# Products of zeros beside batch 0's attention, and its first transfers in a new order

## The chip, the cores and the metric

One core of one Trainium2 chip. The metric is the time of one execution in device microseconds (us), as the median over runs. The profiles and traces are of single executions; their span runs from the first to the last instruction and is about 1.8 us shorter than the time (390.0 us against 391.85 us for the kernel before). In the profiles PE is TensorE, PEld its weight loads, DVE VectorE, ACT ScalarE, POOL GpSimd, SP the sync engine; a q behind a name (SPq) is that engine's sequencer, which issues the transfers.

## The reference

Causal attention with a bias from a running sum, then layer normalisation and a two-layer MLP with a residual:

```python
q, k, v: (8, 8, 576, 64)   s: (8, 8, 576)        # batches, heads, positions, head size
scores = q @ k.T / 8
cum    = cumsum(maximum(s, 0))
scores = where(causal, -1e9, scores + minimum(-(cum_i - cum_j), 0))
attn   = softmax(scores);   x = attn @ v          # heads side by side: (8, 576, 512)
xn     = (x - mean) / sqrt(var + 1e-6) * g_ln
out    = x + relu(xn @ w_ch1) @ w_ch2             # 512 -> 2048 -> 512
```

## The kernel before

Each batch's attention is interleaved with the MLP of the batch ahead of it, so that TensorE has MLP products to do while ScalarE takes exponentials. Batch 0 has no batch ahead of it: its eight heads run without MLP work beside them. That is the stretch in question.

The bias is carried by four extra rows under the 64 rows of k and q (KA = 68): the running sum, split into three bf16 parts, c_hi, c_mid and c_lo, and its partner rows. For the first batches these rows are written by DMA, in "sets" of four heads. k and q come in "pairs" of heads: loaded, cast to bf16, turned by TensorE's transposes, copied into kq.

```python
ps_s, ps_m, ps_t, ps_o      # PSUM pools: 3 + 2 + 2 + 1 banks; ps_m is the MLP's
...
def ld_cast_pair(g):                                   # k and q of two heads, cast on the way
    ... nc.gpsimd.dma_start(out=ready[kind, g][0:QP], in_=pair_src(kind, g))
def ld_v(b, t):                                        # 128 positions of v, all heads
    ... nc.sync.dma_start(out=tmp[:pn], in_=v[b, :, t*P : t*P+pn, :].rearrange("h s d -> s h d"))
def ld_w1(c):                                          # a 512 KB piece of the weights, as bf16
    nc.gpsimd.dma_start(out=w1_bf[:, :, sl], in_=w1_r[:, :, sl])

def aug(gam, eng, last=None):                          # bias rows of a set of four heads
    r0 = gam * G
    i = gam % 2
    eng.dma_start(out=kq[i][D + 1 : D + 2, 0, :, 0:S], in_=c_hi[r0 : r0 + G, :])
    ...                                                # three more rows

def pre(n):                                            # ahead of head n
    ...
    elif n == 2:
        ld_w1(0)
        v_edges(1)
        ld_v(1, 0), ld_v(1, 1), ld_v(1, 2), ld_v(1, 3), ld_v(1, 4)
    elif n == 3:
        ld_cast_pair(5)
    elif n == 4:
        cast_v(1, 0, "pool")
        cast_v(1, 1, "pool")
    elif n == 5:
        ld_w1(1)
        cast_v(1, 2, "pool")
        cast_v(1, 3, "pool")
        cast_v(1, 4, "pool")
    ...
    if n % 4 == 0 and 2 <= n // 4 + 1 < 2 * NPE:
        aug(n // 4 + 1, nc.gpsimd)                     # n = 4: set 2, heads 8 to 11

for n in range(BH):                                    # heads in order
    b, h = n // H, n % H
    pre(n)
    if n < 10:
        scores(b, h)                                   # sa, sb, sc; ends in exponentials into er
        if h % 2 == 0:
            scores_d(b, h // 2)                        # tail diagonal; masked by GpSimd (er)
        if n % 2 == 0 and n < 8:
            g = n // 2 + 1
            qk_pair(g, "dve", "dve" if g % 2 else "act")
        if n == 9:
            for t in range(NF):
                ln_tr(0, t)
            queue += batch_units(0)                    # MLP of batch 0 starts
        if n > 1:
            pv_next()                                  # pot: attn @ v of head n - 2
        if n == 8:
            pv_next()
            qk_pair(5, "act", "act")
```

The casts of batch 1's v by GpSimd in `pre(6)` or earlier stand ahead of the mask of head 6's tail in `scores_d`, and GpSimd ran them in that order.

The softmax here doesn't subtract the row's maximum and nothing guards it: scores larger than these inputs give would overflow.

## Time and profile before

| | before |
|---|---|
| time, median of 3 (lowest to highest) | 393.23 us (392.23 to 393.25) |
| span in the profile | 390.0 us |
| scores of head 0, of head 8, first MLP product start at | 13.07, 39.65, 50.97 us |
| from the first MLP product to the end | 339.0 us |

The prediction below shows the page's clock row and TensorE's timeline. The sync engine's timeline (start, duration, engine, line, what, how many) and GpSimd's:

```profile
11.16 22.95 SPq L132 DMA_DIRECT2D vtmp<-in_v_dram  x10
```

What the stages cost (columns as in the prediction's windows):

```profile
13.07:39.65 26.58, 23.89 (x218) 17.60 (x219) 14.93 (x31) 17.16 (x32) 22.27 (x42) 1.00 1.15 193
39.65:50.97 11.32, 7.66 (x105) 5.88 (x101) 9.41 (x33) 7.27 (x14) 5.23 (x10) 0.80 0.67 108
```

TensorE looks full in heads 0 to 7 (23.89 of 26.58 us) only because its products take nearly twice as long there (from sa to the next product 0.40 us at 37.22, 0.22 us at 39.65); the printed clock of 1.00 is the value before the first record and means nothing.

### The profile page before, as it was taken

Reading aid. Unit: us, or ns where it says so; the run is one execution under the profiler, and the core shown is the slowest. Engines: PE = TensorE matmul, PEld = TensorE weight load, DVE = VectorE, ACT = ScalarE, POOL = GpSimd, SP = SyncE. Lnnn points to the kernel's source line nnn. Section 1 sums busy time; section 2 is a strip of 40 time slices with the busy share of each in tenths; the row PEclk is TensorE's granted clock in tenths of the full one; section 3 lists DMA queues with packets and bytes.
Section 4 is the critical chain, followed back from the end, with each engine's and each line's share of the span. In section 5 each row is a group of like instructions: output and inputs, shape, how many; then the busy total and the mean of one; then the engine's idle time right before and its main releaser. Section 6 shows DMA issues by size and latency. Waiting matters only on the chain.

```text
span 390.0 us, 8129 instructions
## 1 busy us (share of the span) xinstructions
PE 360.7 (92%) x2959; PEld 199.4 (51%) x2959; DVE 202.5 (52%) x530; ACT 189.7 (49%) x359; POOL 177.6 (46%) x473
## 2 busy tenths in 40 slices
PE   1598699897999999999999999999999979999994
PEld 0376555454555555555555555655555534444441
DVE  7347745859643745484437545843665483212211
ACT  3476758574685356436743774277337400411400
POOL 5897359465656264636466656454742110000000
PEclk9999879999999999999999999999999989999998
DMA  8999799256886898749896998599820011002013
GB/s 190 223 155 206 132 129 152 30 105 155 184 180 125 143 242 184 173 118 234 180 166 158 236 177 195 141 213 170 195 92 4 2 54 55 2 28 81 2 34 73
DMA packets 148335, 51.84 MB, mean 133 GB/s; under 512 B 134696, under 2 KB 143496, under 8 KB 148296
## 3 DMA queue, kind: packets, MB, share of 16 engines
q1 hardware_dynamic: 139168, 44.07, 51.9%
q0 software_dynamic: 9120, 7.25, 12.5%
q8 instruction: 23, 0.38, 0.4%
q14 instruction: 16, 0.13, 0.1%
q10 hardware_dynamic: 8, 0.00, 0.0%
HBM read 37.11 MB, written 9.44 MB: 119 GB/s over the span
## 4 chain that ended last, share of the span: by engine, by line
PE 79%; DVE 10%; DMA 5%; ACT 2%; SPq 1%; issue 1%; POOL 0%; ACTq 0%; DVEq 0%
PE py L448 30%; PE ph L430 27%; PE pot L343 7%; PE sa L274 3%; PE sb L274 3%; PE sc L274 3%; DVE xn L401 2%; DVE kq L96 2%; PE trx L417 2%; DMA vtmp<-in_v_dram 2%; PE trqk L227 1%; SPq L149 1%; DMA kq<-c_lo 1%; DMA kq<-rows 1%; ACT er L285 1%
## 5 line engine op out<-in xcount | busy, mean ns | idle before, releaser
L448 PE MATMUL py<-w_bf,hT 128*128 128x512 bf16 x576 | 137.9, 381 | 2.5 <-DVE yo L457 2.2
L430 PE MATMUL ph<-xT,w_bf 128*128 128x512 bf16 x512 | 122.7, 381 | 1.2 <-DVE hT L438 1.0
L440 ACT ACTIVATE hT<-ph 128x512 bf16<-128x512 f32 x107 | 64.0, 598 | 83.4 <-PE ph L430 82.7
L430 PEld LDWEIGHTS <-w_bf 128*128 128x128 bf16 x576 | 52.1, 98 | 55.2 <-issue 5.6
L448 PEld LDWEIGHTS <-hT 128*128 128x128 bf16 x576 | 52.1, 98 | 52.5 <-issue 3.6
L285 ACT ACTIVATE er<-sa 128x512 bf16<-128x512 f32 x64 | 38.1, 596 | 79.2 <-PE sa L274 48.1
L293 POOL TENSOR_SCALAR_AFFINE_SELECT er<-er 128x128 bf16<-128x128 bf16 x216 | 59.5, 300 | 31.2 <-ACT er L285 31.0
L438 DVE TENSOR_SCALAR hT<-ph 128x512 bf16<-128x512 f32 x37 | 25.6, 691 | 58.0 <-PE ph L430 55.2
L161 POOL CAST rows<-rowtmp 128x512 bf16<-128x512 f32 (+1 forms) x50 | 30.5, 610 | 48.9 <-DMA rowtmp<-in_q_dram 46.2
L274 PEld LDWEIGHTS <-kq 68*128 68x128 bf16 x440 | 34.7, 102 | 34.6 <-POOL v_bf L98 5.5
L343 PEld LDWEIGHTS <-er 128*128 128x128 bf16 x960 | 40.0, 102 | 15.2 <-DVE xm L360 2.1
L351 DVE RECIPROCAL rinv<-pot 128x5 f32<-128x5 f32 x64 | 12.4, 194 | 61.1 <-PE pot L343 60.9
L343 PE MATMUL pot<-v_bf,er 128*128 128x65 bf16 x960 | 42.4, 199 | 1.7 <-DVE xm L360 1.7
L285 ACT ACTIVATE er<-sc 128x512 bf16<-128x512 f32 x64 | 38.9, 608 | 0.3
L285 ACT ACTIVATE er<-sb 128x512 bf16<-128x512 f32 x64 | 38.2, 596 | 0.0
L457 DVE SCALAR_TENSOR_TENSOR yo<-py,rstd,xb 128x512 f32<-128x512 f32 x32 | 23.8, 748 | 25.5 <-PE py L448 20.3
L98 POOL CAST v_bf<-vtmp 128x512 bf16<-128x512 f32 (+1 forms) x40 | 24.3, 616 | 17.4 <-DMA vtmp<-in_v_dram 17.3
L274 PE MATMUL sa<-kq 68*128 68x512 bf16 x64 | 26.5, 414 | 6.1 <-DMA kq<-c_lo 5.4
L353 DVE TENSOR_TENSOR xb<-pot,rinv 128x256 f32<-128x256 f32 x64 | 27.2, 425 | 2.2
L274 PE MATMUL sc<-kq 68*128 68x256 bf16 (+1 forms) x208 | 27.9, 244 | 0.1
L96 DVE COPY kq<-trqk 64x576 bf16<-64x576 bf16 x24 | 19.2, 800 | 14.9 <-PE trqk L227 14.5
L274 PE MATMUL sb<-kq 68*128 68x64 bf16 (+1 forms) x168 | 26.7, 261 | 0.2
(81 smaller groups left out, 301.9 us busy)
## 6 DMA issues: line engine op xcount, KB each, us to landing
vtmp<-in_v_dram SPq DMA_DIRECT2D x32, 256.0 KB, 4.2
out_dram<-yo SPq DMA_DIRECT2D x32, 256.0 KB, 2.2
rowtmp<-in_k_dram SPq DMA_DIRECT2D x40, 128.0 KB, 3.0
rowtmp<-in_q_dram SPq DMA_DIRECT2D x40, 128.0 KB, 3.2
w_bf<-in_moe_w_ch_dram POOLq DMA_DIRECT2D x8, 512.0 KB, 9.2
kp<-in_k_dram POOLq DMA_DIRECT2D x10, 144.0 KB, 4.1
qp<-in_q_dram POOLq DMA_DIRECT2D x10, 144.0 KB, 4.8
vtmp<-in_v_dram SPq DMA_DIRECT2D x8, 128.0 KB, 3.2
```

Of the source, the lines that this page charges most:

```text
L96: nc.vector.tensor_copy(out=out, in_=in_)
L98: nc.gpsimd.tensor_copy(out=out, in_=in_)
L161: nc.gpsimd.tensor_copy(out=r[0:pn, :, :, 0:D], in_=loaded.pop(("rows", gam, t))[0:pn])
L274: nc.tensor.matmul(a[:, c + a0 - q0 : c + a1 - q0], lhsT=k_cols(b, h, kb), rhs=cols, start=True, stop=not (pe_mask and diag),)
L285: nc.scalar.activation(out=e[:, o : o + 512], in_=a, func=ACT.Exp, scale=scale)
L293: nc.gpsimd.affine_select(out=e[:, o : o + P], in_=e[:, o : o + P], compare_op=ALU.is_ge, fill=0.0, base=0, pattern=[[1, P]], channel_mult ...
L343: nc.tensor.matmul(pot[:, t, :], lhsT=e[:, o : o + P], rhs=vv[:, kb, h, :], start=(kb == 0), stop=(kb == last),)
L353: nc.vector.tensor_tensor(out=xb[b][:, :, hs], in0=pot[:, 0:NF, 0:D], in1=rinv[:, 0:NF].unsqueeze(2).to_broadcast([P, NF, D]), op=ALU.mult,)
L430: nc.tensor.matmul(ph, lhsT=w1_bf[:, kd, fb * P : (fb + 1) * P], rhs=xT[:, kd, :], start=(kd == 0), stop=(kd == KD - 1),)
L438: nc.vector.tensor_scalar_max(out=hT[:, fb, :], in0=ph, scalar1=0.0)
L440: nc.scalar.activation(out=hT[:, fb, :], in_=ph, func=ACT.Relu)
L448: nc.tensor.matmul(py[0], lhsT=hT[:, fb, t * P : (t + 1) * P], rhs=w2_bf[:, fb, :], start=(fb == 0), stop=(fb == FB - 1),)
```

## The change

Intent: keep TensorE's clock up in batch 0. Products of zeros fill the time in which it would idle; batch 0's transposes use the MLP's two idle PSUM banks, so that the zeros have a bank to go to; head 0's bias rows are made by TensorE instead of DMA; and the first transfers are put in the order in which they are needed, with the bias rows of the sets moved from GpSimd's queue to the sync engine's.

```diff
+    def keep_warm(n):
+        w = ps_t.tile([P, 512], F32, name="idle", tag="tr")
+        for _ in range(n):
+            nc.tensor.matmul(w, lhsT=zeros[:, 0:P], rhs=zeros, start=True, stop=True)
 ...
-            tr = ps_t.tile([P, S], BF16, name="trqk", tag="tr")
+            if g < 6:
+                tr = ps_m.tile([P, S], BF16, name="trqk", tag="m")
+            else:
+                tr = ps_t.tile([P, S], BF16, name="trqk", tag="tr")
 ...
-    ld_v(0, 0)
-    ld_v(0, 1)
+    for t in range(3):
+        ld_v(0, t)
+    ld_cast_pair(2)
 ...                                # clears of kq[1] moved here from pre(0), on GpSimd and DVE
+    keep_warm(9)
 ...
-    aug(0, nc.gpsimd, nc.scalar)
+    aug(0, nc.sync, h0=1)          # heads 1 to 3 only
+    ld_v(0, 3)
     qk_pair(0, "dve", "act")
+    ...                            # head 0's rows: eight products with a selector into ba, bb,
+    ...                            # copied by DVE and ACT; keep_warm(4) and keep_warm(5) between
+    ld_cast_pair(3)
+    aug(1, nc.sync)
+    ld_w1(0)
 ...
         elif n == 1:
-            aug(1, nc.gpsimd)
             ld_cast_pair(4)
         elif n == 2:
-            ld_w1(0)
+            ld_w1(1)
+        elif n == 3:
             v_edges(1)
+            ld_w1(2)
+        elif n == 4:
+            ld_cast_pair(5)
+        elif n == 5:
+            ld_w1(3)
             ld_v(1, 0), ld_v(1, 1), ld_v(1, 2), ld_v(1, 3), ld_v(1, 4)
-        elif n == 3: ...            # pair 5; casts at 4 and 5; weights at 5, 7, 9, 10, 11
+        elif n == 6:
+            ld_w2(0)
+            cast_v(1, 0, "pool")
+            cast_v(1, 1, "pool")
+        elif n == 7:
+            cast_v(1, 2, "pool")
+            cast_v(1, 3, "pool")
+            cast_v(1, 4, "pool")
 ...
-            aug(n // 4 + 1, nc.gpsimd)
+            aug(n // 4 + 1, nc.sync)
 ...
-                qk_pair(g, "dve", "dve" if g % 2 else "act")
+                qk_pair(g, "dve", "act")
+            if n < 8:
+                keep_warm(2)
 ...
             if n == 8:
                 pv_next()
+                keep_warm(8)
```

More of the change, by code (lines that the diff above doesn't have):

```diff
@@ L87 @@
     xTm = const.tile([P, KD, 512], BF16, name="xTm")
-    c_hi = const.tile([BH, S], BF16, name="c_hi")
-    c_mid = const.tile([BH, S], BF16, name="c_mid")
-    c_lo = const.tile([BH, S], BF16, name="c_lo")
+    c3 = const.tile([BH, 3, S], BF16, name="c3")
+    c_hi, c_mid, c_lo = (c3[:, j, :] for j in range(3))
+    zeros = const.tile([P, 512], BF16, name="zeros")
+    ones = const.tile([BH, S], BF16, name="ones")
+    pick = const.tile([BH, 4, P], BF16, name="pick")
     def copy_on(eng, out, in_):
@@ L188, in ld_w2, with aug @@
         )
-    def aug(gam, eng, last=None):
-        r0 = gam * G
+    def aug(gam, eng, h0=0):
+        r = slice(gam * G + h0, gam * G + G)
         i = gam % 2
-        eng.dma_start(out=kq[i][D + 1 : D + 2, 0, :, 0:S], in_=c_hi[r0 : r0 + G, :])
-        eng.dma_start(out=kq[i][D : D + 1, 1, :, 0:S], in_=c_hi[r0 : r0 + G, :])
-        eng.dma_start(out=kq[i][D + 2 : D + 3, 0, :, 0:S], in_=c_mid[r0 : r0 + G, :])
-        (last or eng).dma_start(
-            out=kq[i][D + 3 : D + 4, 0, :, 0:S], in_=c_lo[r0 : r0 + G, :]
-        )
+        eng.dma_start(out=kq[i][D : D + 1, 1, h0:G, 0:S], in_=c_hi[r, :])
+        for j in range(3):
+            eng.dma_start(out=kq[i][D + 1 + j : D + 2 + j, 0, h0:G, 0:S], in_=c3[r, j, :])
     def bias_rows():
@@ L504 @@
         ld_pair("q", g)
-    ld_v(0, 0)
-    ld_v(0, 1)
+    for t in range(3):
+        ld_v(0, t)
+    ld_cast_pair(2)
     ONE2 = 1.0019378662109375
     NEG2 = -1.0058441162109375
+    nc.vector.memset(zeros.bitcast(F32), 0.0)
     nc.vector.memset(warm, 0.0)
     nc.scalar.activation(out=warm[:, 1:2], in_=warm[:, 0:1], func=ACT.Exp)
+    keep_warm(9)
     nc.vector.memset(c_one, 1.0)
+    nc.vector.memset(pick.rearrange("p j m -> p (j m)").bitcast(F32), 0.0)
+    for j in range(3):
+        nc.vector.memset(pick[0:1, j, j + 1 : j + 2], 1.0)
+    nc.vector.memset(pick[0:1, 0, 32:33], 1.0)
+    nc.vector.memset(pick[0:1, 3, 0:1], -1.0)
+    nc.vector.memset(ones.bitcast(F32), ONE2)
     nc.vector.memset(kq[0][0:KA, 0, :, S:SP], 0.0)
     nc.vector.memset(kq[0][D:KA, 1].bitcast(F32), ONE2)
+    nc.vector.memset(kq[1][0:KA, 0, :, S:SP], 0.0)
     make_identity(nc, ident)
@@ L526 @@
     nc.gpsimd.memset(kq[0][D : D + 1, 0].bitcast(F32), NEG2)
+    nc.gpsimd.memset(kq[1][D : D + 1, 0].bitcast(F32), NEG2)
+    nc.gpsimd.memset(kq[1][D:KA, 1].bitcast(F32), ONE2)
     def v_edges(i):
@@ L544 @@
     nc.vector.tensor_tensor(out=c_lo, in0=c_in, in1=c_mid, op=ALU.subtract)
-    aug(0, nc.gpsimd, nc.scalar)
+    aug(0, nc.sync, h0=1)
+    ld_v(0, 3)
     qk_pair(0, "dve", "act")
-    ld_v(0, 2)
-    ld_v(0, 3)
+    ba = ps_s.tile([P, 512], F32, name="ba", tag="s")
+    bb = ps_s.tile([P, 512], F32, name="bb", tag="s")
+    for j, src in ((3, ones), (0, c_hi), (1, c_mid), (2, c_lo)):
+        if j == 2:
+            keep_warm(4)
+        nc.tensor.matmul(
+            ba, lhsT=pick[:, j, :], rhs=src[:, 0:512], start=(j == 3), stop=(j == 2)
+        )
+    for j, src in ((3, ones), (0, c_hi), (1, c_mid), (2, c_lo)):
+        nc.tensor.matmul(
+            bb[:, 0:TL], lhsT=pick[:, j, :], rhs=src[:, 512:S], start=(j == 3), stop=(j == 2)
+        )
+    nc.vector.tensor_copy(out=kq[0][D:KA, 0, 0, 0:512], in_=ba[0:4])
+    nc.scalar.copy(out=kq[0][D : D + 1, 1, 0, 0:512], in_=ba[32:33])
+    nc.vector.tensor_copy(out=kq[0][D:KA, 0, 0, 512:S], in_=bb[0:4, 0:TL])
+    nc.scalar.copy(out=kq[0][D : D + 1, 1, 0, 512:S], in_=bb[32:33, 0:TL])
+    keep_warm(5)
     cast_pair("k", 1, "pool")
@@ L551 @@
     ld_v(0, 4)
-    ld_cast_pair(2)
+    ld_cast_pair(3)
+    aug(1, nc.sync)
+    ld_w1(0)
     v_edges(0)
@@ L562, in pre @@
         if n == 0:
-            ld_cast_pair(3)
-            nc.gpsimd.memset(kq[1][D : D + 1, 0].bitcast(F32), NEG2)
-            nc.gpsimd.memset(kq[1][D:KA, 1].bitcast(F32), ONE2)
-            nc.gpsimd.memset(kq[1][0:KA, 0, :, S:SP], 0.0)
             nc.vector.memset(mhalf, -0.5)
         elif n == 1:
-            aug(1, nc.gpsimd)
             ld_cast_pair(4)
         elif n == 2:
-            ld_w1(0)
+            ld_w1(1)
+        elif n == 3:
             v_edges(1)
+            ld_w1(2)
[3 more added lines that the diff above has]
+            ld_w1(3)
             ld_v(1, 0), ld_v(1, 1), ld_v(1, 2), ld_v(1, 3), ld_v(1, 4)
-        elif n == 3:
-            ld_cast_pair(5)
-        elif n == 4:
+        elif n == 6:
+            ld_w2(0)
             cast_v(1, 0, "pool")
             cast_v(1, 1, "pool")
-        elif n == 5:
-            ld_w1(1)
+        elif n == 7:
             cast_v(1, 2, "pool")
@@ L584, in pre @@
             cast_v(1, 4, "pool")
-        elif n == 6:
+        elif n == 8:
             ld_cast_pair(6)
-        elif n == 7:
-            ld_w1(2)
-            ld_w1(3)
+            ld_w2(1)
         elif n == 9:
+            ld_w2(2)
+        elif n == 10:
             ld_cast_pair(7)
-            ld_w2(0)
-        elif n == 10:
-            ld_w2(1)
-            ld_w2(2)
-        elif n == 11:
             ld_w2(3)
```

## The prediction

> **What bounds the kernel now.** I read the page first: TensorE (PE) is busy 92% of the span, and the windows put nearly all of its slack at the front. From 100 us on it works 282.5 of 290 us, so a microsecond gained before the MLP starts should reach the end whole. The changed lines all act before that start.
>
> Page of the kernel before, busy tenths in slices of 9.75 us:
>
> ```profile
> PE   1598699897999999999999999999999979999994
> PEclk9999879999999999999999999999999989999998
> ```
>
> PE is low in slices 1 to 7 and full after; the clock row dips around 39 to 58 us. That row is deceptive at the front: the first clock record stands at 39.54 us and the row shows full speed where there is none. The matmuls tell the truth. PE's timeline, start, duration, tile:
>
> ```profile
> 13.07 0.59 PE L274 MATMUL sa<-kq 68*128 68x512 bf16 x1 [5.36 <-DMA kq<-c_lo]
> ...
> 16.21 0.63 PE L274 MATMUL sa<-kq 68*128 68x512 bf16 x1
> ...
> 37.22 0.62 PE L274 MATMUL sa<-kq 68*128 68x512 bf16 x1
> ...
> 39.65 0.38 PE L274 MATMUL sa<-kq 68*128 68x512 bf16 x1
> ...
> 49.70 0.62 PE L274 MATMUL sa<-kq 68*128 68x512 bf16 x1
> ...
> 50.97 1.91 PE L430 MATMUL ph<-xT,w_bf 128*128 128x512 bf16 x4
> ...
> 56.09 0.38 PE L274 MATMUL sa<-kq 68*128 68x512 bf16 x1
> ```
>
> The same 512-column product takes 0.6 us up to 38 us, 0.38 us at 39.65, 0.62 us again at 49.7, and 0.38 us from 56 on. So all of batch 0's attention but its last heads runs at half clock, and so do the first products of the MLP. The sa lines also give the pace: head 0 starts at 13.07 after PE waited 5.36 us for a bias row (c_lo) to come by DMA, head 1 at 16.21, head 8 at 39.65 (3.35 us a head), and the first MLP product at 50.97.
>
> What makes the clock change can be read by cutting the windows at its records (columns: window, PE, PEld, DVE, ACT, POOL busy, granted clock, DMA share, GB/s):
>
> ```profile
> 22.47:25.88 3.41, 3.40 (x37) 2.49 (x35) 1.63 (x5) 3.01 (x5) 3.30 (x8) 1.00 0.91 121
> ...
> 36.12:39.54 3.42, 3.42 (x42) 2.80 (x41) 1.96 (x5) 2.89 (x5) 1.84 (x4) 1.00 1.27 213
> 39.54:42.95 3.41, 2.48 (x53) 2.01 (x51) 2.33 (x10) 2.00 (x5) 2.13 (x5) 1.00 1.25 213
> 42.95:46.36 3.41, 1.79 (x25) 1.20 (x23) 3.35 (x14) 3.05 (x4) 0.00 (x0) 1.00 0.80 132
> 46.36:49.78 3.42, 2.31 (x28) 2.22 (x29) 2.83 (x7) 1.71 (x4) 2.02 (x3) 0.50 0.01 2
> 49.78:53.19 3.41, 3.41 (x15) 1.44 (x13) 1.18 (x4) 1.68 (x4) 3.41 (x8) 0.50 0.80 95
> 53.19:56.60 3.41, 3.41 (x28) 1.89 (x27) 0.98 (x2) 2.18 (x5) 1.24 (x4) 1.00 1.13 158
> ```
>
> Full clock follows the windows that PE filled (36.12 to 39.54, 49.78 to 53.19). Half clock follows one filled to 1.79 us, while one of 2.48 us kept the clock. Counting columns at the clock in force instead of modelled ends, I get 0.99 and 1.00 of the window before the two rises, 0.94 for 22.47 to 25.88, which did not raise it, 0.59 in the window that held it and 0.41 in the one that lost it. Rising seems to need an almost full window, holding about half of one.
>
> [...]
>
> **The change, part by part.**
>
> Start. The bias rows of head 0 no longer come by DMA but by eight products with a selector, copied out by VectorE (DVE) and ScalarE (ACT). DVE gets some 1.4 us of extra clears ahead of the scan, less the 0.6 us that it idled for c_in: c_lo ends near 8.95 instead of 8.1. Then the 1.6 us copy of k, about 0.65 and 0.15 us of bias copies (estimates from the 0.6 us of 512-column copies): head 0 starts near 11.5, not 13.07. Heads 1 to 3 still need rows by DMA, now from the sync queue. Before, c_lo took 4.9 us from issue to use. With c_lo issued near 9.2 behind less traffic (the last v tiles now follow it), I take head 1 at 13.9, not 16.21: 2.3 us gained.
>
> Heads 1 to 8. From the warm stretch at 39.65: scores 0.9 us of PE, diagonal tail 0.06 a head, transposes 0.25, pv 0.47, plus two zero products at 0.216 us (512 columns, from the 0.22 us spacing of sa): 2.1 us a head. ACT: three exponentials at 0.49 us spacing, 0.13 for the tail, and q's copy 1.61 us per pair of heads, which the change now always gives to ACT: 1.5 + 0.13 + 0.8 = 2.4 us. DVE: 0.8 for k's copy, 0.85 for pv's output, up to 0.7 for statistics: 2.35 us. Hence ACT, not PE, sets the pace, at 2.43 us; with in-order losses I take 2.6. Seven heads: 18.2 us instead of 23.44, 5.2 us gained, so head 8 at 32.1 instead of 39.65. The padding costs PE 42 x 0.216 = 9 us, but in time that it would have idled.
>
> Head 8 to the MLP. Before, 11.3 us. DVE's chain (statistics, xn 2.66 us, copies of xT) stays. What goes is half clock on the last transposes, one pv and one scores (about 1.2 us). The eight zero products, 1.7 us, lie in DVE's shadow. So 10.0 us: first MLP product at 42.1, against 50.97: 8.9 us.
>
> MLP's first products. 50.97 to 53.19 ran at half clock: 2.2 us of work worth 1.1.
>
> Sum: 8.9 + 1.1 = 10.0 us. I take off 0.3 us for the new order of transfers (below): 393.2 - 9.7 = 383.5 us.
>
> **The rivals.**
>
> The clock stays low at first. [...] Then head 0 starts near 13.5 and the gain at the start shrinks to about 1 us: 384.5. If zeros did not count as activity at all, 9 us of padding would be paid at half clock: about 395. Nothing in this trace shows products of zeros, so I give that 3 in 100.
>
> DMA takes the place of the clock. Up to 46 us the 16 engines moved 50 us of packet time at a share of at most 1.27. By the packets' times a 512 KB weight piece takes 3.2 us of sixteen engines, a pair of k and q 2.0, a v tile 1.5. Before head 8 needs its pair 5, the queue must carry four pairs, three weight pieces, batch 0's v and the first k and q: 30 us of it, 23.5 us at 1.27, plus 2.5 us to begin: 26 us, needed at 32. That fits, by six microseconds. Tighter are batch 1's v tiles: issued near 23, landing 7 to 9 us later under load as before, and their GpSimd casts stand ahead of the mask that head 6's pv needs at head 8. A stall of 0 to 3 us is possible: up to 386.
>
> ACT takes all of the relief: with 2.9 us a head the gain falls by 2 us, to 385.5. For it speaks that copies of q from pairs 1 and 3 now land on ACT.
>
> Gain lost later: PE idled only 2.3 us between 80 and 100, and 0.2 us from 100 to 300, so there is little slack to absorb it. I think it stays.
>
> **Range and chances.** The good end: no stall, 2.45 us a head, head 1 at 13: about 379.5. The bad end: late clock plus a v stall plus a slow ACT: 388.5. The line for faster by over 2% is 385.4; the centre lies 1.9 us below it and two of the rivals reach it. I say 0.67 faster, 0.31 same, 0.02 slower.
>
> **What would show it.** Right: sa of heads 1 to 9 at 0.38 us, heads 2.4 to 2.7 us apart, first ph near 42 at full clock, no half clock until the tail, the stage from there to the end as long as before less about 1 us, and the wait for kq's c_lo gone from head 0. Wrong: sa still 0.6 us past 16 us; waits on v tiles, pair 5 or weights near heads 6 to 9; a wait for weights at the start of MLP; or a longer stage after it.

The sum: 8.9 + 1.1 - 0.3 = 9.7 us, and so 383.5; 13.5 and 384.5 stand as estimates. Behind some figures stand these measured ones, all of the kernel before. Each record of the clock but the last lasts a whole multiple of 3.41 us (6.83, 6.83, 266.24, 3.41 and 64.85), which is the length of the windows. GpSimd took 0.53 us to issue a bias row and 2.1 us for a set (20.56 to 22.64). The first DMA packets moved at 2.1 us, for which 2.5 us "to begin" are allowed. The 1.4 us of extra clears are an estimate; DVE's clears took 0.54 us for 576 columns and 0.17 us for 128.

## More of the kernel before

```profile
27.19 1.18 POOL L98 CAST v_bf<-vtmp 128x512 bf16<-128x512 f32 x2
...
31.42 1.73 POOL L98 CAST v_bf<-vtmp 128x512 bf16<-128x512 f32 x3
...
35.97 0.28 POOL L316 TENSOR_SCALAR_AFFINE_SELECT er<-er 64x128 bf16<-64x128 bf16 x1 [1.59 <-ACT er L315]
```

Behind batch 0's five, the sync engine issues ten more v tiles, batch 1's and then batch 2's, with no bias rows among them; batch 1's begin at 11.16, well ahead of the first weight piece, which GpSimd issues at 23.93. (The 22.95 us hold waits for staging buffers too, so they can't be set beside issue times further down.) GpSimd casts batch 1's five tiles without any wait for them (a wait would stand in brackets), and the mask of head 6 waits only for its own exponential. All is early, because the heads are slow.

## The result, and the profile after

The changed kernel took 396.89 us, median of 4 runs (396.69 to 397.83); the kernel before, in the same rounds, 392.73 us (392.06 to 393.25). The ratio is 1.011, 95% interval 1.009 to 1.014: within 2%, but slower, and outside the predicted range. A ratio here and below is the mean time of one kernel's runs over that of the kernel before's runs of the same rounds, so it is not quite the ratio of the medians. Executions over 1.5% slower than the fastest of the same kernel are left out of the means.

The page of the changed kernel, tenths in slices of 9.9 us:

```profile
PE   5986189899799999999999999999999979999995
PEclk9699579999999999999999999999999999999999
```

PE, at 8 and 9 from the second slice on, falls to 6 and 1 in the fourth and fifth, and the clock goes down with it. TensorE's timeline says what stood there:

```profile
14.57 0.63 PE L276 MATMUL sa<-kq 68*128 68x512 bf16 x1
...
17.13 0.38 PE L276 MATMUL sa<-kq 68*128 68x512 bf16 x1
...
35.69 0.38 PE L276 MATMUL sa<-kq 68*128 68x512 bf16 x1
...
46.84 0.29 PE L345 MATMUL pot<-v_bf,er 128*128 128x65 bf16 x2 [9.49 <-POOL er L318]
...
48.89 3.60 PE L501 MATMUL idle<-zeros 128*128 128x512 bf16 x8
...
58.15 1.03 PE L432 MATMUL ph<-xT,w_bf 128*128 128x512 bf16 x4
```

Heads 1 to 8 run at full clock (0.38 us a product) and on average 2.65 us apart, as intended: (35.69 - 17.13) / 7. (Heads 2 and 3 start 4.90 us apart, as TensorE waits 0.53 us for casts of batch 0's v and 1.26 us for a mask behind them; the others are closer.) Then pot, head 6's product with v, waits 9.49 us for er, the mask that GpSimd makes. The chain of waits, read backwards from there, gives the cause:

```profile
28.96 16.92 DMA vtmp<-in_v_dram
45.88 0.05 issue
45.93 0.62 POOL v_bf L100
46.55 0.25 POOL er L318
46.80 0.05 issue
46.84 0.30 PE pot L345 x2
```

The mask itself takes 0.25 us. It stands behind the cast of batch 1's second v tile, and that tile landed at 45.88. The windows cut at the clock's records show what the stall did to the clock:

```profile
36.41:39.82 3.41, 0.94 (x19) 0.72 (x17) 1.09 (x6) 1.62 (x4) 0.00 (x0) 1.00 1.23 192
39.82:43.23 3.41, 0.00 (x0) 0.00 (x0) 0.00 (x0) 0.00 (x0) 0.61 (x1) 0.50 1.21 197
```

After a window with PE busy 0.94 us the clock is at half from 39.82 on, and it does not come back before 53.47. So the eight zero products, which should have hidden in DVE's shadow at 1.7 us, took 3.60 us once work resumed.

Why the v tiles were late takes some more views. The sync engine's timeline and its longest wait up to 60 us (total, times, longest):

```profile
25.26 0.58 SPq L197 DMA_DIRECT2D kq<-c  x1
...
27.86 17.90 SPq L134 DMA_DIRECT2D vtmp<-in_v_dram  x5
```

```profile
SPq L197 <- PE sc L276: 6.9, 1, 6.9
```

The v loads stand behind set 2's bias rows (kq<-c), which now go by the sync engine too and wait 6.9 us for heads 0 to 3 to be done with kq. So the first v load is issued at 27.86. While the sync engine waited, the DMA engines had next to nothing to do: GpSimd, which issues the weights, stood too, 6.00 us up to 21.91, for the last of batch 0's v, and issued its next weight pieces only at 25.28, 27.25, 29.52 and 30.29, side by side with v. Queues from 22 to 26 us (packets, MB, share of 16 engines):

```profile
q0 software_dynamic: 77, 0.06, 14.0%
q1 hardware_dynamic: 38, 0.06, 3.8%
```

From 28 to 32 us, just after the first v issue:

```profile
q0 software_dynamic: 481, 0.48, 92.1%
q1 hardware_dynamic: 14, 0.01, 0.9%
```

And from 36 to 40 us:

```profile
q0 software_dynamic: 671, 0.59, 90.0%
q1 hardware_dynamic: 671, 0.17, 32.3%
```

q0 carries what GpSimd issues: the weights, in packets of 1024 bytes, and pairs of k and q, in packets of 768; q1 carries v. From 36 to 40 us both moved exactly as many packets, and in every single microsecond from 34 to 43 the two counts lie within 3 of each other. What rule shares the engines out, no run here shows. A packet of v in the profile is 256 bytes (0.17 MB / 671), one of q0 here about 880 on average (0.59 MB / 671), so equal counts give v 22% of the bytes. A v tile is 256 KB, 1024 packets: at 671 in 4 us it takes 6.1 us.

This rate does not account for all of the lateness. The trace has v's first packet only at about 32.9 us, 5.0 us after the first v issue; until then q1 moved the 16 larger packets of set 2's rows and little else, as the window from 28 to 32 us shows. Why they took so long beside q0 is open.

### The profile page after: what moved, and what is told of

It reads as the page before. It is cut to its first block, busy times and chain, and to the rows that moved or that the text cites. A ratio compares the mean times of both kernels' runs of the same rounds, so it can differ in the third digit from the quotient of the medians.

```text
span 396.1 us, 8233 instructions
## 1 busy us (share of the span) xinstructions
PE 366.0 (92%) x3009; PEld 196.9 (50%) x3009; DVE 203.3 (51%) x537; ACT 192.2 (49%) x365; POOL 165.8 (42%) x449
## 3 DMA queue, kind: packets, MB, share of 16 engines
q1 hardware_dynamic: 139352, 44.18, 51.0%
## 4 chain that ended last, share of the span: by engine, by line
PE 61%; DMA 14%; DVE 8%; POOL 6%; issue 5%; SPq 3%; ACT 3%; ACTq 0%; POOLq 0%; DVEq 0%
PE py L450 23%; PE ph L432 23%; DMA vtmp<-in_v_dram 11%; PE pot L345 4%; SPq L151 3%; PE sc L276 2%; PE sb L276 2%; PE sa L276 2%; POOL v_bf L100 2%; POOL er L295 2%; DVE xn L403 2%; ACT er L287 1%; PE trx L419 1%; DMA kq<-rows 1%; PE trqk L229 1%
## 5 line engine op out<-in xcount | busy, mean ns | idle before, releaser
L450 PE MATMUL py<-w_bf,hT 128*128 128x512 bf16 x576 | 136.5, 379 | 2.5 <-DVE yo L459 2.2
L295 POOL TENSOR_SCALAR_AFFINE_SELECT er<-er 128x128 bf16<-128x128 bf16 x216 | 58.5, 294 | 36.3 <-ACT er L287 36.2
L345 PE MATMUL pot<-v_bf,er 128*128 128x65 bf16 x960 | 40.6, 194 | 12.9 <-POOL er L318 10.8
L345 PEld LDWEIGHTS <-er 128*128 128x128 bf16 x960 | 37.9, 98 | 28.4 <-POOL er L318 11.0
L353 DVE RECIPROCAL rinv<-pot 128x5 f32<-128x5 f32 x64 | 12.4, 193 | 71.3 <-PE pot L345 71.1
L163 POOL CAST rows<-rowtmp 128x512 bf16<-128x512 f32 (+1 forms) x50 | 30.9, 618 | 42.1 <-DMA rowtmp<-in_q_dram 38.8
L276 PEld LDWEIGHTS <-kq 68*128 68x128 bf16 x440 | 33.2, 98 | 27.8 <-issue 4.3
L96 ACT COPY kq<-trqk 64x576 bf16<-64x576 bf16 x28 | 22.5, 803 | 24.5 <-PE trqk L229 24.3
L276 PE MATMUL sa<-kq 68*128 68x512 bf16 x64 | 25.0, 390 | 1.3 <-ACT er L287 1.3
L276 PE MATMUL sc<-kq 68*128 68x256 bf16 (+1 forms) x208 | 25.6, 234 | 0.3
L276 PE MATMUL sb<-kq 68*128 68x64 bf16 (+1 forms) x168 | 24.9, 249 | 0.6 <-DMA kq<-rows 0.3
```

What stands on the lines that cost most here:

```text
L163: nc.gpsimd.tensor_copy(out=r[0:pn, :, :, 0:D], in_=loaded.pop(("rows", gam, t))[0:pn])
L276: nc.tensor.matmul(a[:, c + a0 - q0 : c + a1 - q0], lhsT=k_cols(b, h, kb), rhs=cols, start=True, stop=not (pe_mask and diag),)
L295: nc.gpsimd.affine_select(out=e[:, o : o + P], in_=e[:, o : o + P], compare_op=ALU.is_ge, fill=0.0, base=0, pattern=[[1, P]], channel_mult ...
L345: nc.tensor.matmul(pot[:, t, :], lhsT=e[:, o : o + P], rhs=vv[:, kb, h, :], start=(kb == 0), stop=(kb == last),)
L450: nc.tensor.matmul(py[0], lhsT=hT[:, fb, t * P : (t + 1) * P], rhs=w2_bf[:, fb, :], start=(fb == 0), stop=(fb == FB - 1),)
```

## The experiments

The theory: heads 6 to 8 stall because batch 1's v is starved, first by its place behind set 2's rows on the sync queue, then by weight pieces that move beside it. Rivals: the zeros do not pay or do harm; the wait is only GpSimd's order, with the casts ahead of the mask; or it is the total load on the engines, and any order would stall somewhere. Runs 1 to 4 shared one chip, 5 to 12 a second, 13 to 16 a third, 17 and 18 a fourth. All gave correct results. Ratios are to the kernel before; the kernels are edits of the changed one unless it is said otherwise.

**e1: batch 1's v ahead of set 2's rows.**

```diff
         elif n == 2:
+            ld_v(1, 0), ld_v(1, 1), ld_v(1, 2), ld_v(1, 3), ld_v(1, 4)
             ld_w1(1)
         elif n == 5:
             ld_w1(3)
-            ld_v(1, 0), ld_v(1, 1), ld_v(1, 2), ld_v(1, 3), ld_v(1, 4)
```

> Changed kernel, with batch 1's five v loads put ahead of the second half's bias rows (set 2) on the sync queue; nothing else moves. Theory A (the v tiles are issued too late, at 27.9 us, because set 2's rows in front of them wait for heads 0 to 3, and then starve beside the weight pieces; their GpSimd casts hold up head 6's mask and so pv): the 9.5 us wait of pv on the mask goes, first ph product comes near 47 instead of 58 us, total 385 to 388 us. Rival B (the loss comes from the zero products or a clock lost in the middle): no change, 396 to 397 us, the clock still drops near 40 us. Rival C (the DMA engines are simply full up to 46 us, order doesn't matter): the wait moves to another tile (pair 5 or weights), total 392 to 396 us.

Measured: 384.46 us (383.8 to 385.33), ratio 0.979 (0.974 to 0.984). One moved line is worth 12.4 us. Its TensorE and its sync engine:

```profile
35.13 0.38 PE L276 MATMUL sa<-kq 68*128 68x512 bf16 x1
...
45.57 1.03 PE L432 MATMUL ph<-xT,w_bf 128*128 128x512 bf16 x3
```

```profile
18.12 7.31 SPq L134 DMA_DIRECT2D vtmp<-in_v_dram  x5
```

Head 8 starts where it did (35.13 against 35.69), and the first MLP product follows 10.44 us later instead of 22.46. The five v loads take 7.31 us to issue instead of 17.90 (one issue alone took 7.44 there). From 20 to 24 us v's queue moved 2882 packets, nearly all of them v's, beside 26 of the other: 1024 of them in 1.4 us, against the 6.1 us above. The transfers, and the order of the weights among themselves, are those of the changed kernel; only v's place has moved. So the total load is not what stalls it: that rival falls here.

**e2: the rows of sets 2 and on back on GpSimd's queue**, v left in its place.

```diff
-            aug(n // 4 + 1, nc.sync)
+            aug(n // 4 + 1, nc.gpsimd)
```

> Changed kernel, with bias row sets 2 to 5 issued by GpSimd as before the change, set 0 and 1 still by sync. The v loads of batch 1 keep their place in the program but have no waiting row in front of them on the sync queue. Theory A: they issue near 18 to 24 us, ahead of most weight pieces; most of the 9.5 us wait goes; 386 to 390 us (GpSimd pays 2.1 us a set again). Rivals B and C: 394 to 397 us.

Measured: 392.39 us (390.11 to 393.59), ratio 0.998 (0.993 to 1.004). v was issued from 17.71, as early as in e1, and the wait at head 6 is gone. In its place GpSimd issued the rows late, and TensorE waited 1.95 us for them at head 8; the clock fell at 24.0 and again at 41.1, and the first MLP product started at 50.78. So the place on the sync queue is one cause, but taking it away by this route makes another wait.

**e3: GpSimd's order alone.** The two casts go behind the mask; v is as late as in the changed kernel.

```diff
         elif n == 6:
             ld_w2(0)
-            cast_v(1, 0, "pool")
-            cast_v(1, 1, "pool")
         elif n == 7:
+            cast_v(1, 0, "pool")
+            cast_v(1, 1, "pool")
             cast_v(1, 2, "pool")
```

> Changed kernel, transfers untouched, but the first two v casts of batch 1 stand behind the mask of heads 6 and 7 on GpSimd. Theory A in the form that the order on GpSimd carries the stall: pv of heads 6 and 7 no longer waits, but the tiles still land near 46 us and head 8's pv needs them and pair 6 and the later weights are issued behind the casts: about half comes back, 389 to 394 us, with a shorter wait of PE at head 8's pv for a v cast. If the lateness of the tiles alone decides: 395 to 397 us. Rival B: 396 to 397 us.

Measured: 394.77 us (392.45 to 396.35), ratio 1.006 (1.000 to 1.013). TensorE's waits:

```profile
47.64 0.31 PE L345 MATMUL pot<-v_bf,er 128*128 128x65 bf16 x5 [0.53 <-POOL v_bf L100]
...
50.50 0.24 PE L345 MATMUL pot<-v_bf,er 128*128 128x65 bf16 x1 [2.55 <-POOL er L318]
```

Head 6's product, which belongs to batch 0 and needs none of these tiles, no longer waits. The lateness turns up at head 8, the first product that does need batch 1's v, and the first MLP product starts at 51.81 and at half clock. The order on GpSimd is how the late tiles reach TensorE; it is not why they are late. That rival falls.

**e4: e1 without the zeros** (one of 42 products is left, so that the tile is written).

```diff
-        for _ in range(n):
+        for _ in range(1 if n == 9 else 0):
```

> Run e1 with all but one of the 42 zero products taken out. If the zeros earn what the prediction says (clock up from head 1 on): 5 to 9 us slower than e1, sa products at 0.6 us for most of batch 0 and a clock record that first rises past 30 us. If the clock rises by itself from the real work: within 2 us of e1. If the zeros cost more than they bring: faster than e1.

Measured: 389.49 us (388.93 to 390.32), ratio 0.992 (0.987 to 0.997); 5.0 us slower than e1 on the same chip. The clock rises first at 33.65:

```profile
33.16 0.62 PE L276 MATMUL sa<-kq 68*128 68x512 bf16 x1
...
35.31 0.38 PE L276 MATMUL sa<-kq 68*128 68x512 bf16 x1
```

Without zeros the heads run at half clock up to 33 us, as before the change. In e1, with the zeros, sa takes 0.38 us from 16.87 on: here products of zeros brought the clock up. They also cost something: head 0 starts at 13.45 in e4 and at 14.51 in e1.

**e5: the TensorE part alone, on the kernel before**: the transposes in the MLP's banks, q's copies on ACT, 42 zero products (the 18 of the start as 9 and 9). Transfers and head 0's rows as before.

> The kernel before, with TensorE's part alone: transposes of batch 0 in the MLP's banks, q's copies all on ScalarE, 42 zero products (9 at the start, 9 before head 0, 2 a head, 8 at head 8). Order of transfers and the bias rows of head 0 as before the change. If the zeros earn their time by themselves: 385 to 389 us, sa at 0.38 us from head 2 on, no stall of pv. If the earlier order of transfers was only good enough for the slow clock (the DMA bound takes over): 389 to 393 us, with waits on pair 4, pair 5 or rows.

Measured: 388.16 us (386.8 to 392.96, one run of them slow), ratio 0.987 (0.982 to 0.992). Alone this half gains about 5 us (1.3%); TensorE then waits 1.51 us (head 4) and 0.83 us (head 8) for bias rows by DMA.

**e6 and e7: two attempts to improve e1's start.** In e6 GpSimd's clears of kq[1] go behind its casts of pair 1. In e7 a v tile of batch 0 goes ahead of heads 1 to 3's rows, and the first weight piece behind batch 0's v casts.

```diff
 e6                                                  e7
-    nc.gpsimd.memset(kq[1][D : D + 1, 0]...)        -    aug(0, nc.sync, h0=1)
-    nc.gpsimd.memset(kq[1][D:KA, 1]...)                  ld_v(0, 3)
 ...                                                 +    aug(0, nc.sync, h0=1)
     cast_pair("q", 1, "pool")                       ...
     ld_v(0, 4)                                      -    ld_w1(0)
     ld_cast_pair(3)                                      v_edges(0)
+    nc.gpsimd.memset(kq[1][D : D + 1, 0]...)             for t in range(NT): cast_v(0, t, "pool")
+    nc.gpsimd.memset(kq[1][D:KA, 1]...)             +    ld_w1(0)
```

> Run e1 with GpSimd's two long clears of the second key buffer moved from the start behind the casts of pair 1. Theory: head 0 came 3 us later than predicted because VectorE's cumulative-sum chain ran slowly beside GpSimd's clears (1.10 us for the cast to c_hi, 0.45 us in the kernel before; 1.16 us against 0.45 us for the first step). Then the chain ends 1.5 to 2 us earlier and head 0 starts 0.7 to 1.5 us earlier; total 383 to 384.5 us. Rival: the zero products at low clock in front of head 0 set its start; then the chain is faster but head 0 starts within 0.5 us of e1 and the total is within 0.6 us.

> Run e1 with batch 0's fourth v tile ahead of the bias rows on the sync queue and the first weight piece behind batch 0's casts. Theory: pv of head 0 in e1 waits some 2 us in all for the v casts (the tiles were issued at 13 us behind rows that waited for the cumulative sums, then lay beside pair 3 and a weight piece): those waits shrink to under 0.5 us; total 1 to 2 us below e1. Rival: ScalarE sets the pace there and absorbs it: within 0.7 us of e1.

Measured: both lost what e1 had gained. e7 took 396.23 us (394.93 to 397.82), ratio 1.009 (1.004 to 1.015). e6 had two fast runs, 390.0 and 392.98 us, ratio 0.997 (0.990 to 1.005). e7's sync engine and TensorE:

```profile
17.78 20.73 SPq L134 DMA_DIRECT2D vtmp<-in_v_dram  x5
```

```profile
44.19 0.58 PE L276 MATMUL sa<-kq 68*128 68x512 bf16 x1 [9.48 <-DMA kq<-c]
```

v starts to be issued as early as in e1 (17.78) and takes 20.73 us instead of 7.31, because weight pieces now meet it: 626 packets of each queue from 28 to 32 us. It is not the first piece alone. In e1 GpSimd issued that piece at 12.47 and the second not until 24.73, as it stood 5.33 us for batch 0's v; in e7 it stands for 0.98 us only, and issues the first piece at 17.22 and four more from 20.19 to 28.05, while v is being loaded. The victim is new, though: set 2's rows now stand behind v on the sync queue, so head 8's scores wait 9.48 us. So e1 was right partly by luck of timing; a shift of some four microseconds undid it. A faster engine off the critical path triggered its transfers earlier, into those of another. The starvation is the cause, and who waits depends on who stands behind v.

**e8: two weight pieces held back** until v is cast, v left where the change put it.

```diff
         elif n == 5:
-            ld_w1(3)
             ld_v(1, 0), ld_v(1, 1), ld_v(1, 2), ld_v(1, 3), ld_v(1, 4)
         elif n == 6:
-            ld_w2(0)
 ...
         elif n == 7:
             ...                                     # casts
+            ld_w1(3)
+            ld_w2(0)
```

> Changed kernel, v loads of batch 1 left where they are (late, behind the waiting rows of set 2), but the fourth weight piece of the first matrix and the first of the second issued only after batch 1's casts. Theory: lateness of issue (27.9 us instead of about 18) and starvation beside weight pieces both make the stall. If starvation makes most of it: the 9.5 us wait falls under 4 us and the total to 388 to 392 us. If late issue alone makes it: the wait stays 8 to 10 us, total 396 to 398 us.

Measured: 391.31 us (389.16 to 391.72), ratio 0.995 (0.991 to 1.000). The wait at head 6 is 2.77 us instead of 9.49, the five loads take 11.75 us to issue. Fewer weights beside the same late v recover most of the wait. So starvation counts by itself, apart from the late issue. That the remaining wait is the late issue's is argued, not shown, by this run.

**e9 to e12: pacing.** In e9, e7 with v at head 1 and the later weight pieces one to a head from head 5 on, but the first piece still behind batch 0's v casts. e10 adds e6's edit. e11 is the changed kernel with v at head 1 and the same pacing, first piece in its place. e12 is e1 once more.

```diff
 e11
         elif n == 1:
+            ld_v(1, 0), ld_v(1, 1), ld_v(1, 2), ld_v(1, 3), ld_v(1, 4)
             ld_cast_pair(4)
 ...                                # w1(1), w1(2), w1(3), w2(0), w2(1), w2(2), w2(3)
                                    # at heads 5, 6, 7, 8, 9, 10, 11
```

> Run e7 (396 us, head 8 waited 9.5 us for bias rows of set 2 behind starved v tiles on the sync queue) with batch 1's v loads one head earlier and the weight pieces after the first spread out as in the kernel before: one each at heads 5, 6, 7, 8, 9, 10 and 11. Theory (256-byte v packets share the engines packet for packet with 1 KB weight packets[...]): the 9.5 us wait goes, no wait of PE on a transfer over 1 us before the MLP, first ph near 43.5 us, total 381 to 384 us. Rival (the rows or tiles are late for another reason, such as their own issue): a wait of 5 us or more stays and the total is over 390 us.

> Run e9 with GpSimd's two long clears moved behind the casts of pair 1, as in e6, where the cast to c_hi took 0.45 us instead of 1.10 and head 0 started 0.5 us earlier. Theory: with the transfers paced nothing makes an earlier GpSimd harmful; 0.3 to 1 us below e9, 380.5 to 383.5 us. If earlier issues still collide: a wait for rows or tiles returns and it is slower than e9.

> Changed kernel with only batch 1's v loads moved to head 1 and the weight pieces spread as in e9; order of batch 0's v tiles and the clears as in the change. Expected between e1 and e9: waits of pv on batch 0's casts stay (about 2 us, partly hidden), 382.5 to 385 us.

> Run e1 again on the chip of e9 to e11, to compare them by the same runs: 383.5 to 385.5 us, no wait of PE on a transfer over 1.5 us before the MLP. Since e6 and e7 lost 10 us to a shift of only some 4 us in GpSimd's issues, a slow execution of it among the fast ones would show that e1's order is near that edge.

(The "packet for packet" of e9's theory is the count of the changed kernel, 671 packets of each queue from 36 to 40 us, and of e7, 626 of each from 28 to 32.)

Measured:

| | median us (lowest to highest) | ratio (95%) | issue of the five v loads |
|---|---|---|---|
| e9 | 392.02 (389.19 to 393.43) | 0.998 (0.993 to 1.003) | 12.17 us |
| e10 | 388.43 (384.35 to 392.64, two of six slow) | 0.984 (0.978 to 0.991) | profile slow |
| e11 | 385.62 (384.35 to 386.82) | 0.982 (0.978 to 0.986) | 7.47 us |
| e12 | 386.61 (384.16 to 389.63) | 0.985 (0.979 to 0.991) | 7.44 us |

In e9 weight pieces still meet v (issued at 16.59 and 27.31; the last v cast comes at 38.60, after a wait of 2.69 us), and head 8 waits 2.23 us for its rows. In e11 hardly any weights meet v, and by the ratios it is not apart from e1. e12's spread of 5.5 us, against 1.5 us in e1's first runs, fits an order that holds only while the timing does; the slow end has no profile. What the profiles do show is one lost window of the clock. In e11 and e12, waits for batch 0's v at heads 2 and 3 (0.64 and 1.26 us in e12) left a window with TensorE busy 1.61 and 1.52 us, the clock was at half for the next one (24.83 to 28.24 in e12), and the first MLP product came at 47.59 and 47.92; e1 had a wait of 1.36 us there too, but its window (22.28 to 25.69) still held 2.08 us and kept the clock, and that product came at 45.57. That this makes the spread is not shown.

**e13: all weight pieces behind batch 1's v.** If starvation is the cause, e7's start must be harmless once no weight piece can meet v.

```diff
 e7's place of ld_v(0, 3), and
-    ld_w1(0)                        # at the start
         elif n == 1:
+            ld_v(1, 0), ld_v(1, 1), ld_v(1, 2), ld_v(1, 3), ld_v(1, 4)
         elif n == 2:
+            ld_cast_pair(4)
 ...                                # w1(0..3) at heads 5 to 8, w2(0), w2(1) at 9, w2(2) at 10, w2(3) at 11
```

> Run e9 (392 us, head 8 waited 2.2 us for rows in the profiled run) with all weight pieces behind batch 1's v loads: the first at head 5, then one a head, two at head 9; pair 4 one head later. Theory of starvation: v tiles issue without being held (under 2 us each), rows of set 2 land before head 8 asks, no wait of PE on a transfer over 1 us before the MLP, first ph near 44 to 46 us, 381 to 384.5 us. Rival (rows late for another reason): the wait at head 8 stays at 2 us or more, 388 us or more. Risk: weights come too late and ph waits for w_bf.

Measured: 384.94 us (383.81 to 385.81), ratio 0.981 (0.978 to 0.983). No wait for batch 1's v is left, and of those for rows only one of 0.55 us, before head 1:

```profile
17.79 7.80 SPq L134 DMA_DIRECT2D vtmp<-in_v_dram  x5
```

The five loads take 7.80 us instead of e7's 20.73, and the first MLP product starts at 44.72; the first weight piece is issued at 26.98. So weights beside v are what made e7's v late. This run alone doesn't rule out the total load, since the weights' bytes leave the stretch with it; e1, which moves no transfer but v, does.

**e14 to e18: what is left at the start**, all on e13. e14 loads pair 2 behind the casts of pair 1 instead of first of all; e15 drops the 18 zero products before head 0; e16 has e6's clears behind the casts of pair 1; e17 is e14 and e16 together; e18 is e17 with two zero products instead of five right before head 0.

```diff
 e14  -    ld_cast_pair(2)                 # at the very start
      +    ld_cast_pair(2)                 # behind cast_pair("q", 1, "pool")
 e15  -    keep_warm(9) ... keep_warm(4) ... keep_warm(5)
 e18  -    keep_warm(5)
      +    keep_warm(2)
```

> e13 with pair 2's load moved from the very start to behind the casts of pair 1. If the early load delays q of pair 0 (its cast began at 7.5 us, at 6.2 in the kernel before): q's cast moves to about 6.2 us; head 0 starts at most 0.5 us earlier because the sum chain still sets it; total within 1 us of e13.

> e13 without the 18 zero products before head 0 (the two a head and the eight at head 8 stay). If the start's zeros are paid at low clock in front of head 0: head 0 starts at about 13.5 us instead of 14.5, as in e4, but the clock rises later, at head 3 to 6; net within 2 us of e13. If they earn the clock of the first heads, e15 is 1 to 3 us slower.

> e13 with GpSimd's two long clears behind the casts of pair 1 as in e6: cast to c_hi 0.45 us, head 0 at about 14.0 instead of 14.5 us, 0.3 to 1 us faster than e13 if no transfer collides; slower with a new wait for rows or tiles if it does.

> e13 with both pair 2's load and the two clears behind the casts of pair 1. If their effects add: VectorE's chain ends near 8.7 us, head 0 at about 13 us, total 382 to 384 us, within 1 us of e16 or below it. If they don't (the zero products hold head 0): head 0 near 13.8, total as e16.

> e17 with two zero products instead of five directly before head 0. If those hold head 0: it starts 0.6 to 1.2 us earlier than in e17, total up to 1 us less, unless the clock then rises one 3.4 us window later, which would give it back. If VectorE's and ScalarE's copies hold it: the same start.

Measured:

| | median us (lowest to highest) | ratio (95%) | head 0, head 1 start at |
|---|---|---|---|
| e13 | 384.94 (383.81 to 385.81) | 0.981 (0.978 to 0.983) | 14.79, 17.40 |
| e14 | 384.0 (383.0 to 385.12) | 0.978 (0.975 to 0.982) | 14.27, 16.82 |
| e15 | 387.02 (384.26 to 388.83) | 0.984 (0.981 to 0.988) | 14.11, 18.24 |
| e16 | 383.65 (382.73 to 386.1) | 0.978 (0.975 to 0.982) | 13.86, 16.47 |
| e17 | 384.65 (383.9 to 385.22) | 0.979 (0.976 to 0.982) | 12.87, 16.47 |
| e18 | 386.08 (383.61 to 387.44) | 0.984 (0.981 to 0.987) | 12.81, 16.39 |

The 18 zeros at the start are worth 2.1 us by the medians (e15 against e13) although they delay head 0; the intervals of the two ratios just overlap. e16 brings head 0 forward by 0.9 us for a reason that DVE's timeline shows. The first cast of the running sum, in the changed kernel and in e16:

```profile
6.87 1.10 DVE L562 CAST c<-c_sc 64x576 bf16<-64x576 f32 x1
```

```profile
6.89 0.45 DVE L560 CAST c<-c_sc 64x576 bf16<-64x576 f32 x1
```

In the changed kernel one of GpSimd's clears ran from 6.50 to 7.66, beside the cast; in e16 it is elsewhere. So the cast took 1.10 us with a clear beside it and 0.45 us without; why is not shown. e17 stacks both gains and is no faster. Head 1 then waits for its rows:

```profile
15.42 0.19 PE L310 MATMUL sd<-kq 68*128 68x64 bf16 x1 [1.45 <-DMA kq<-c]
```

It starts at 16.47 in e16 and in e17 alike; and in e17 the clock fell at 16.30 for a window, so that the products of heads 1 and 2 took 0.63 us. Three fewer zeros in e18 bought 0.06 us at head 0 and lost 1.4 us in the median; the intervals of their ratios overlap.

e16, at 383.65 us the fastest, is faster than the kernel before by 2.2% (1.8 to 2.5%) and, by the two ratios to it, than the changed one by some 3% (0.978 / 1.011); e14, e1, e13 and e17 lie within 1.3 us of it, too close to rank.

## Why the prediction was wrong

What it said of the zeros and of the pace was right. The term that failed is the stall between head 8 and the MLP: 0 to 3 us forecast, 9.49 us measured. Beside it the start was 3.2 us late. By its own steps (us; a column is one profile, a row one stage):

| | predicted | before | after | e1 | e13 |
|---|---|---|---|---|---|
| head 0 starts | 11.5 | 13.07 | 14.57 | 14.51 | 14.79 |
| head 0 to 1 | 2.4 | 3.14 | 2.56 | 2.36 | 2.61 |
| head 1 to 8 | 18.2 | 23.44 | 18.56 | 18.26 | 16.88 |
| head 8 to first MLP product | 10.0 | 11.32 | 22.46 | 10.44 | 10.44 |
| first MLP product at | 42.1 | 50.97 | 58.15 | 45.57 | 44.72 |
| from there to the end | about 1.1 less | 339.0 | 337.9 | 336.5 | 337.7 |

*The clock and the pace: right.* Sa of heads 1 to 8 at 0.38 us (head 9's, after the stall, took 0.49), 2.65 us a head against 2.6. That figure's closeness is partly luck, as it holds the two waits for batch 0's v. The mechanism, that ScalarE would set the pace, is seen best where no such wait is left: in e13 a head takes 2.41 us (16.88 / 7), against 2.43 that the prediction gave ScalarE; TensorE is busy 14.53 of these 16.88 us. In the changed kernel's 18.56 us ScalarE is busy 16.80 and TensorE 15.22. The chance of 3 in 100 that zeros do not count was well placed: e4 against e1 shows 5.0 us for them.

*The start: wrong, by 3.2 us at head 1 (17.13 against 13.9), and the prediction's rival took that up only in part.* Its late-clock rival had head 0 near 13.5; measured, the clock was up at 5.69, lost again at 9.10 after a window with TensorE busy 1.11 us, and up for good only at 15.93. Head 0 came at 14.57: the first product still took 0.63 us, DVE's chain was slower while GpSimd's clears ran (its first step took 1.16 us against 0.45 before, the cast 1.10 against 0.45), q's cast came 1.4 us later than before (7.53 against 6.17), as pair 2 was now loaded ahead of it (5.94 in a run with pair 2 late, e14), and the zero products ran at half clock right up to head 0. In no run did the first MLP product come as early as 42.1: e16 reaches 44.59, e14 44.27 and e18, the earliest, 44.18.

*Head 8 to the MLP: this step failed.* The prediction named the right wait, word for word: "batch 1's v tiles: issued near 23, landing 7 to 9 us later under load as before, and their GpSimd casts stand ahead of the mask that head 6's pv needs at head 8. A stall of 0 to 3 us is possible: up to 386." The stall was 9.49 us, and 2.5 us more are left over (22.46 - 10.44 - 9.49). Of these the half clock that followed shows 1.9 us in the eight zeros (3.60 against 1.7); that the rest went to it too is argued. Three inputs of that term were off. The issue came at 27.86, not 23, as the rows ahead of v on the same queue wait for heads 0 to 3. The tiles did not land 7 to 9 us later: the first was cast 13.2 us after its issue began (41.09), and the second landed 16.9 us after its own; 5.0 us of the first passed before any packet of v moved, which is not explained here. And the sum over the transfers, "23.5 us at 1.27", treated the sixteen engines as one pool whose share any transfer can have, while between 22 and 26 us they stood nearly empty (14.0% and 3.8%) and from 36 to 40 us v got 22% of the bytes. The prediction also missed that moving the rows' issues changed what stood behind them: v, for the 6.9 us that they waited.

*From the MLP on: right.* 1.1 us predicted, 337.9 against 339.0.

*The sum.* The first MLP product was 16.05 us later than predicted: 3.23 at head 1, 0.36 of pace, 12.46 after head 8. The time was 13.4 us above the prediction; the other 2.7 us are the choice of runs and what the prediction had taken off elsewhere. The profiled run of the changed kernel was the longest of its four, 0.9 us above its median; that of before was 1.4 us below the 393.2 that the prediction started from. With the stall gone, e1 ran in 384.46 us, inside the range and 1 us from the centre, at a start three microseconds later than predicted and with a stage after it that was 1.4 us shorter than in the changed kernel. So e1's closeness is partly two errors against each other.

*The clock.* "Rising seems to need an almost full window, holding about half of one", which the prediction read from windows of the kernel before, does not fit others. In the changed kernel full clock followed a window with PE busy 3.02 of 3.42 us (2.27 to 5.69); it did not follow two with PE busy 3.41 of 3.41 us, by modelled ends and at half clock (9.10 to 12.51 there, 9.77 to 13.18 in e7). (Counted in columns as the prediction did, 0.43 us for 512 at half clock, as in the four ph from 50.97 to 52.67 of the kernel before, the first window comes to about 0.8 and the two to about 0.9, by estimate; so that does not settle it either.) What decides there stays open. Of windows at full clock, those with 0.94 us, 1.52 (e12) and 1.61 (e11) were followed by half clock, those with 2.08 (e1) and 2.48 (the kernel before, 39.54 to 42.95) were not. But half clock also followed one with 2.40 us in the changed kernel (73.95 to 77.37), and it did not follow one with 1.50 us there (323.13 to 326.54) and one with 1.94 us in the kernel before (90.74 to 94.15). So a share that holds the clock is not shown either. Also open are why e12 spread over 5.5 us, and the 5.0 us before v's first packet.

## What to carry to other kernels

Before putting loads "in order of need", write down for each queue what every load stands behind and what that waits for: a queue that waits for compute holds back the loads behind it while the engines idle (here v by 6.9 us, with the DMA queues at 14.0% and 3.8% from 22 to 26 us). When two queues are busy, count packets as well as bytes: here both moved 671 in 4 us, so that v with its 256 bytes a packet got 22% of the bytes beside packets of about 880. So keep bulk weights out of the stretch in which small-packet loads are urgent. And a faster stage brings its consumers forward: each load that was comfortably early at the old pace has to be placed again. So does a faster engine off the critical path, whose own transfers then start earlier (e7).
